# Two steps of a float64 unpacking on GpSimd and a scaling on ScalarE, in a recurrence and gated-MLP kernel whose order is written out by hand

## The chip, the cores and the metric

One core of a Trainium2 chip. The metric is the device time in microseconds of the whole kernel, the median of three runs. The engines are called PE (TensorE), DVE (VectorE), ACT (ScalarE), POOL (GpSimd) and SP (SyncE, which issues the DMAs here).

## The reference

Two parts follow each other. The first is a recurrence over 768 time steps for 4 batches of 8 heads, each with a 40 x 40 state. The second takes its output, 320 wide, through a projection to 1024, a convolution of three taps over time, a gate, and a projection back to 320:

```python
for t in range(S):                                   # S = 768; state is (B, H, 40, 40)
    y[:, :, t] = einsum("bhd,bhde->bhe", r_t, state)
    Sa = einsum("bhde,bhe->bhd", state, a_t)
    state = state * w_t[:, :, None, :] - einsum("bhd,bhe->bhde", Sa, b_t) \
            + einsum("bhd,bhe->bhde", v_t, k_t)
x = y.transpose(0, 2, 1, 3).reshape(B, S, 320)
h = maximum(x @ w_in, 0)                             # w_in: 320 x 1024
gate = 1 / (1 + exp(-conv3(h, conv_w)))              # three taps over time, per channel
out = (h * gate) @ w_out                             # w_out: 1024 x 320
```

w_in, conv_w and w_out lie in device memory as float64.

## The kernel before

**Recurrence.** Time is cut into 24 chunks of 32 steps, and two chunks make a pair (12 pairs). For a pair, the columns w, a, k, b are loaded and turned, a scan gives the decays, and `scores` gives the products within each chunk. `solve_in` sends them through DRAM into the layout bb, and `solve` (lines 480 and 486) inverts 32 x 32 triangular matrices, 128 of them at once, in 31 steps of two operations each: a product into st and a sum into xx. The even pairs' solves run on VectorE, the odd pairs' on GpSimd. `chain` then carries the state from chunk to chunk: TensorE's pp (L514, from the old state s and from v), ScalarE's psb (L527), TensorE's pu, ScalarE's u, TensorE's pn, the sum into the new s on VectorE (L562), and its scaling by wc in four operations on GpSimd (L568). For the outputs `rturn` makes rp (L579) and rt, `turn` makes vt and ut (L593), `sturn` makes sn, `pairs` takes pm (L411) into ms on VectorE (L614), `outputs` makes ysb, and `hats` makes khat and bhat (L451). `finish` splits the result in a high part xh (ScalarE) and a low part xl (GpSimd, L667).

**Second part.** It runs in 12 windows of 64 steps, each in four quarters of the 1024 channels (`moe_in`, `moe_out`), between the chunks of the recurrence. The matrix products are made of high and low parts too, so that each weight exists twice, as wih and wil (w_in) and as woh and wol (w_out).

**The weight pieces.** float64 is unpacked on the chip from its two 32-bit words, once, piece by piece, in 23 pieces: twelve of w_in (wi00 to wi23: the first digit is the group of 120 rows, the second the quarter of columns), one of conv_w (cv), eight of w_out (wo0 to wo7) and two for its last 64 columns (wp0, wp1). A piece is 120 or 128 partitions by 256 columns, cv 24 by 128. It has four steps: a load; `from_f64`, eight VectorE operations on integers (lines 217 to 235); the conversion to the high part on ScalarE (L253); the subtraction that gives the low part on GpSimd (L255). In `from_f64`, e holds the exponent, t the sign, the exponent and the upper mantissa, and m the remaining mantissa bits. Line 228 takes m out of the low word, line 230 clears t where the number is too small, line 231 (the mask) leaves in e only t's power of two, line 232 multiplies m, scaled by 2^-44, by that power, and line 235 adds the product to t. For cv a transposition on TensorE (pc, L269) takes the place of the last steps. The raw words lie in a buffer "gh", e and t in one half each of a buffer "gl" (named ...q in the trace), m in another "gl" (named ...s), with four buffers a tag. All weight pieces are built in the first third of the run, while solve 1 and solve 3 (pairs 1 and 3) run on GpSimd and solve 2 on VectorE.

**The order.** Nothing is reordered by a scheduler. A string ORDER lists the steps of all parts (`we3` is one step of weight piece 3, `so1` some steps of solve 1, `ch4` one step of the chain), `put` names which steps must stand ahead of which, and `emit_all` gives the steps out in that order. Each engine then works off its own queue strictly in order, and an instruction that waits holds everything behind it on its engine. ORDER is written on the level of steps: when a step has one more instruction on an engine, that instruction stands in the engine's queue where the step stands.

Of the kernel before, what the change touches and what calls it, by code (L numbers as in the profile page):

```python
# [8 lines left out]
F32 = mybir.dt.float32  # L9
# [3 lines left out]
AF = mybir.ActivationFunctionType  # L13
ALU = mybir.AluOpType
# [98 lines left out]
def tile_decay_delta_attention_then_conv_gate_moe(  # L113
# [13 lines left out]
    nc = tc.nc  # L127
# [30 lines left out]
    def quad(i):  # L158
        return slice(C * i, C * i + C)
# [7 lines left out]
        out=hmask, in_=hmask, compare_op=ALU.is_ge, fill=0.0,  # L167
# [3 lines left out]
        out=hmask, in_=hmask, compare_op=ALU.is_ge, fill=0.0,  # L171
# [4 lines left out]
    for q in range(B):  # L176
        nc.gpsimd.affine_select(
            out=tri[quad(q), :], in_=tri[quad(q), :],
# [6 lines left out]
        out=trin[:, 1, 0], in0=tri, scalar1=-1.0, scalar2=None, op0=ALU.mult  # L185
# [3 lines left out]
    for z in range(2):  # L189
        zs = slice(z * 64, z * 64 + 64)  # L190
        nc.gpsimd.affine_select(
            out=xini[zs], in_=xini[zs], compare_op=ALU.is_equal, fill=0.0,
# [20 lines left out]
    def from_f64(raw, e, t, m):  # L213

        lo, hi = raw[..., 0], raw[..., 1]
        V = nc.vector
        V.tensor_scalar(
            out=e, in0=hi, scalar1=20, scalar2=0x7FF,
            op0=ALU.logical_shift_right, op1=ALU.bitwise_and,
        )  # L220
        V.tensor_scalar(
            out=t, in0=hi, scalar1=3, scalar2=0x3FFFFFFF,
            op0=ALU.logical_shift_left, op1=ALU.bitwise_and,
        )
        V.scalar_tensor_tensor(
            out=t, in0=hi, scalar=-(1 << 30), in1=t, op0=ALU.bitwise_and, op1=ALU.bitwise_or
        )
        V.tensor_scalar(out=m, in0=lo, scalar1=8, scalar2=None, op0=ALU.logical_shift_right)
        tf, ef = t.bitcast(F32), e.bitcast(F32)
        V.scalar_tensor_tensor(out=tf, in0=e, scalar=896.5, in1=tf, op0=ALU.is_ge, op1=ALU.mult)  # L230
        V.tensor_scalar(out=e, in0=t, scalar1=-(1 << 23), scalar2=None, op0=ALU.bitwise_and)
        V.scalar_tensor_tensor(
            out=ef, in0=m, scalar=2.0**-44, in1=ef, op0=ALU.mult, op1=ALU.mult
        )
        V.tensor_tensor(tf, tf, ef, ALU.add)
        return tf

    def words(nm):
# [5 lines left out]
    def piece(nm, load, dsth, dstl, rows, shape):  # L244
        raw, e, t, m = words(nm)
        raw = raw[:rows]
        load(raw)
        yield
        f = from_f64(raw.rearrange("p (c z) -> p c z", z=2), e[:rows], t[:rows], m[:rows])
        if len(shape) == 2:  # L250
            f = f.rearrange("p (a c) -> p a c", a=shape[0])
        yield
        nc.scalar.copy(dsth, f)  # L253
        yield
        nc.gpsimd.tensor_tensor(dstl, f, dsth.bitcast(F32), ALU.subtract)  # L255
        yield

    def conv_piece():
        NCV = KW * NF
        craw, ce, ct, cm = words("cv")  # L260
        nc.sync.dma_start(craw[:NCV, :256], conv_w.rearrange("k (f p) -> (k f) p", p=256))
        yield
        cf = from_f64(
            craw[:NCV, :256].rearrange("p (c z) -> p c z", z=2),
            ce[:NCV, :128], ct[:NCV, :128], cm[:NCV, :128],
        )
        yield
        pc = psM.tile([128, 512], F32, tag="M", name="pc")
        nc.tensor.transpose(pc[:, :NCV], cf, ident[:NCV, :NCV])  # L269
        nc.scalar.copy(cw.rearrange("p k f -> p (k f)"), pc[:, :NCV])  # L270
        yield
        yield
# [730 lines left out]
```

## Time and profile before

| | |
|---|---|
| median of three runs | 711.65 us (707.79, 711.65, 715.09) |
| the profiled execution | 708.08 us, span 706.4 us |
| mean granted TensorE clock | 0.906 |
| TensorE, matmuls | 560.7 us busy, 79% of the span |
| VectorE | 538.4 us, 76% |
| ScalarE | 350.7 us, 50% |
| GpSimd | 353.2 us, 50% |
| data moved by DMA | 53.40 MB, 76 GB/s on average |

A row of a timeline gives the start in us from the span's start, the length of one instruction (or of a group, with xN), the engine, the line, the operation, its output and inputs with sizes, and in brackets the idle time of the engine just before it with what ended it. A row without brackets began as soon as its engine's previous instruction let it. A row of the stretches gives busy us of each engine with the number of instructions, the granted clock, the share of the DMA engines, and GB/s.

### The profile page before, as it was taken

Reading aid. Unit: us, or ns where it says so; the run is one execution under the profiler, and the core shown is the slowest. Engines: PE = TensorE matmul, PEld = TensorE weight load, DVE = VectorE, ACT = ScalarE, POOL = GpSimd, SP = SyncE. Lnnn points to the kernel's source line nnn. Section 1 sums busy time; section 2 is a strip of 40 time slices with the busy share of each in tenths; the row PEclk is TensorE's granted clock in tenths of the full one; section 3 lists DMA queues with packets and bytes.
Section 4 is the critical chain, followed back from the end, with each engine's and each line's share of the span. In section 5 each row is a group of like instructions: output and inputs, shape, how many; then the busy total and the mean of one; then the engine's idle time right before and its main releaser. Section 6 shows DMA issues by size and latency. Waiting matters only on the chain. (4 is left out here: it accounts for less than half of the span.)

```text
span 706.4 us, 29930 instructions
## 1 busy us (share of the span) xinstructions
PE 560.7 (79%) x13021; PEld 497.9 (70%) x13021; DVE 538.4 (76%) x1261; ACT 350.7 (50%) x792; POOL 353.2 (50%) x582
## 2 busy tenths in 40 slices
PE   4444764677687898988977996899998977899886
PEld 3334654566576787977866885789887876788775
DVE  6689889998999896657795578987979894456571
ACT  2322244254375455664454664466565546455651
POOL 2001884037786235783234884236985028863321
PEclk9766777997799998989999998999998999999998
DMA  8765456437125344544404446524435025121000
GB/s 139 120 117 108 103 112 102 95 94 144 22 41 107 56 72 79 94 81 82 82 20 89 86 86 106 81 60 69 89 62 91 6 54 94 29 51 32 21 30 19
DMA packets 242402, 53.40 MB, mean 76 GB/s; under 512 B 229000, under 2 KB 238112, under 8 KB 242272
## 3 DMA queue, kind: packets, MB, share of 16 engines
q1 hardware_dynamic: 242272, 51.50, 39.9%
q8 instruction: 102, 1.67, 1.0%
q14 instruction: 28, 0.23, 0.1%
HBM read 38.63 MB, written 10.22 MB: 69 GB/s over the span
## 5 line engine op out<-in xcount | busy, mean ns | idle before, releaser
L729 DVE SCALAR_TENSOR_TENSOR cc<-hb,cw,cc 128x256 f32<-128x256 f32 x192 | 106.3, 575 | 13.7 <-ACT cc L721 10.2
L568 POOL TENSOR_TENSOR s<-s,wc 120x360 f32<-120x360 f32 x88 | 75.8, 891 | 69.4 <-DVE s L562 69.4
L486 POOL TENSOR_TENSOR xx<-xx,st 128x126 f32<-128x126 f32 (+22 forms) x186 | 83.1, 447 | 14.6
L480 POOL TENSOR_TENSOR st<-xx,bb 128x126 f32<-128x126 f32 (+22 forms) x186 | 79.4, 427 | 21.1 <-DMA bb<-bd 8.4
L700 PE MATMUL ph<-xh,wih 120*128 120x256 f32 x288 | 56.6, 306 | 11.3 <-ACT hb L714 11.3
L486 DVE TENSOR_TENSOR xx<-xx,st 128x126 f32<-128x126 f32 (+22 forms) x186 | 54.2, 291 | 6.4
L480 DVE TENSOR_TENSOR st<-xx,bb 128x126 f32<-128x126 f32 (+22 forms) x186 | 53.6, 288 | 7.2 <-DMA bb<-bd 1.7
L736 DVE TENSOR_TENSOR cc<-cc,hb 128x512 f32<-128x512 f32 x48 | 40.8, 857 | 21.7 <-ACT cc L734 21.5
L562 DVE TENSOR_TENSOR s<-pn,s 120x360 f32<-120x360 f32 x88 | 40.6, 522 | 20.6 <-PE pn L549 20.6
L700 PEld LDWEIGHTS ph<-xh,wih 120*128 120x128 f32 x288 | 41.8, 194 | 15.0 <-ACT hb L714 13.1
L734 ACT ACTIVATE cc<-cc 128x512 f32<-128x512 f32 x48 | 30.4, 636 | 43.6 <-DVE cc L729 43.5
L667 POOL TENSOR_TENSOR xl<-xf,xh 120x384 fp32r<-120x384 f32 x24 | 26.8, 1117 | 45.2 <-ACT xh L665 41.5
L721 ACT ACTIVATE cc<-hb,cw 128x256 f32<-128x256 f32 x96 | 43.5, 506 | 8.7 <-DVE hb L712 2.9
L602 PE MATMUL pt<-ident,s 120*120 120x120 f32 x276 | 40.6, 279 | 6.4 <-DVE s L562 3.2
L427 ACT ACTIVATE ap<-ah,hmask 120x384 f32<-120x384 f32 (+1 forms) x72 | 36.6, 576 | 17.4 <-DVE ah L391 10.1
L604 ACT COPY sn<-pt 120x360 f32<-120x360 f32 x92 | 38.9, 471 | 12.2 <-PE pt L602 11.8
L714 ACT ACTIVATE hb<-ph 128x512 f32<-128x512 f32 x48 | 28.8, 600 | 27.2 <-PE ph L700 23.4
L579 ACT ACTIVATE rp<-pr,hmask 120x384 f32<-120x384 f32 x72 | 36.7, 586 | 6.9 <-PE pr L576 6.5
L700 PE MATMUL ph<-xl,wih 120*128 120x256 f32 x192 | 39.3, 287 | 0.0
L533 PE MATMUL pu<-psb,tt 32*32 32x40 f32 x1536 | 22.5, 209 | 19.6 <-ACT psb L527 16.1
L602 PEld LDWEIGHTS pt<-ident,s 120*120 120x120 f32 x276 | 31.2, 143 | 9.0 <-DVE s L562 3.5
L533 PEld LDWEIGHTS pu<-psb,tt 32*32 32x32 f32 x1536 | 18.7, 114 | 24.5 <-ACT psb L527 17.7
(867 smaller groups left out, 1665.9 us busy)
## 6 DMA issues: line engine op xcount, KB each, us to landing
bb<-bd SPq DMA_DIRECT2D x24, 256.0 KB
w<-in_w_dram SPq DMA_DIRECT2D x24, 160.0 KB
a<-in_a_dram SPq DMA_DIRECT2D x24, 160.0 KB
k<-in_k_dram SPq DMA_DIRECT2D x24, 160.0 KB
b<-in_b_dram SPq DMA_DIRECT2D x24, 160.0 KB
r<-in_r_dram SPq DMA_DIRECT2D x96, 40.0 KB
v<-in_v_dram SPq DMA_DIRECT2D x96, 40.0 KB
out_dram<-ob SPq DMA_DIRECT2D x22, 160.0 KB
```

The costliest lines, as they stand in the source:

```text
L480: eng.tensor_tensor(t3, xx[:, 0:nj, i : i + 1].to_broadcast([128, nj, nt]), bb[:, i : i + 1, i + 1 :].to_broadcast([128, nj, nt]), ALU.mult,)
L486: eng.tensor_tensor(xx[:, 0:nj, i + 1 :], xx[:, 0:nj, i + 1 :], t3, ALU.add)
L533: nc.tensor.matmul(pu[quad(bi), hc], tt[quad(bi), c, h, :], psb[quad(bi), hc], start=(h == 0), stop=True, skip_group_check=True,)
L562: nc.vector.tensor_tensor(new, pn[bi][:GR], old[bi], ALU.add)
L568: nc.gpsimd.tensor_tensor(n4, n4, w4, ALU.mult)
L579: nc.scalar.activation(out=rp[:, :, h, :], in_=pr[:GR], func=AF.Copy, scale=hmask[:, h : h + 1])
L602: nc.tensor.transpose(pt[:GR, g, :], old[bi][:, g, :], ident[:GR, :GR])
L604: nc.scalar.copy(sn, pt[:GR])
L700: nc.tensor.matmul(ph[:, j], l[:, fs], x, start=(j == 0 and i == 0), stop=(i == len(passes) - 1), skip_group_check=True,)
L721: nc.scalar.activation(out=cc[:, j], in_=hb[:, j, :, 1 : W + 1], func=AF.Copy, scale=cw[:, 1, f : f + 1],)
L729: nc.vector.scalar_tensor_tensor(out=cc[:, j], in0=hb[:, j, :, x : W + x], scalar=cw[:, x, f : f + 1], in1=cc[:, j], op0=ALU.mult, op1=ALU ...
L736: nc.vector.tensor_tensor(cc, cc, hb[:, :, :, 1 : W + 1], ALU.mult)
```

## The change

In `from_f64` the multiply and the add go from VectorE to GpSimd. GpSimd's multiply has two inputs only, so the factor 2^-44 becomes an operation of its own, on ScalarE, which also takes m from integer to float:

```diff
         V.tensor_scalar(out=m, in0=lo, scalar1=8, scalar2=None, op0=ALU.logical_shift_right)
         tf, ef = t.bitcast(F32), e.bitcast(F32)
+        nc.scalar.activation(out=m.bitcast(F32), in_=m, func=AF.Copy, scale=2.0**-44)
         V.scalar_tensor_tensor(out=tf, in0=e, scalar=896.5, in1=tf, op0=ALU.is_ge, op1=ALU.mult)
         V.tensor_scalar(out=e, in0=t, scalar1=-(1 << 23), scalar2=None, op0=ALU.bitwise_and)
-        V.scalar_tensor_tensor(
-            out=ef, in0=m, scalar=2.0**-44, in1=ef, op0=ALU.mult, op1=ALU.mult
-        )
-        V.tensor_tensor(tf, tf, ef, ALU.add)
+        nc.gpsimd.tensor_tensor(ef, m.bitcast(F32), ef, ALU.mult)
+        nc.gpsimd.tensor_tensor(tf, tf, ef, ALU.add)
         return tf
```

VectorE has six operations a piece instead of eight, ScalarE two instead of one, GpSimd three instead of one. Lines behind the change are numbered one less: L254, L479, L485 and L567 are the former L255, L480, L486 and L568. ORDER, the dependencies and the buffers are as before. The new instructions stand in their queues where the step `from_f64` of the piece stands in ORDER, two steps earlier than the subtraction of the same piece. Three places show it.

GpSimd's queue in the second half of solve 1, before (xx and st belong to the solve, wil to the pieces; the steps 12 to 19 that lie ahead are left out):

```order
L486 TENSOR_TENSOR xx_821<-xx_821,st_19_1165 128x10x12
L255 TENSOR_TENSOR wil<-wi22q,wih 120x256
L480 TENSOR_TENSOR st_20_1398<-xx_821,bb_673 128x121
L486 TENSOR_TENSOR xx_821<-xx_821,st_20_1398 128x11x11
L480 TENSOR_TENSOR st_21_1401<-xx_821,bb_673 128x110
```

The same place in the changed kernel:

```order
L485 TENSOR_TENSOR xx_827<-xx_827,st_19_1173 128x10x12
L233 TENSOR_TENSOR wi22q<-wi22s,wi22q 120x256
L234 TENSOR_TENSOR wi22q<-wi22q 120x256
L254 TENSOR_TENSOR wil<-wi22q,wih 120x256
L233 TENSOR_TENSOR wi03q<-wi03s,wi03q 120x256
L234 TENSOR_TENSOR wi03q<-wi03q 120x256
L233 TENSOR_TENSOR wi13q<-wi13s,wi13q 120x256
L234 TENSOR_TENSOR wi13q<-wi13q 120x256
L479 TENSOR_TENSOR st_20_1409<-xx_827,bb_679 128x121
L485 TENSOR_TENSOR xx_827<-xx_827,st_20_1409 128x11x11
```

Ahead of step 20 of the solve, where one subtraction stood, three pairs now stand as well, those of wi22, wi03 and wi13; further ahead, between steps 11 and 16, stand the pairs of wi02 and wi12.

ScalarE's queue in the same stretch, before, with the engine whose signal each instruction waits for (sn, ap, rp, rt, ut, ysb and khat belong to the recurrence):

```order
L253 CAST wih<-wi22q 120x256 [waits DVE_49]
L579 ACTIVATE rp_1235<-pr_1231,hmask 120x3x128 [waits PE_49]
L579 ACTIVATE rp_1235<-pr_1231,hmask 120x3x128 x2
L584 COPY rt_1239<-pr_1231 120x384
L604 COPY sn_1253<-pt_1249 120x360 [waits PE_49]
L604 COPY sn_1259<-pt_1255 120x360 [waits PE_49]
L593 COPY ut_1265<-put_1261 120x384 [waits PE_49,Activation_49]
L644 COPY ysb_1376<-py_1299 128x320 [waits PE_49,Activation_49]
L451 COPY khat_1378<-pz4k 128x320 [waits PE_49]
```

And in the changed kernel:

```order
L230 ACTIVATE wi22s<-wi22s 120x256 [waits DVE_49]
L252 CAST wih<-wi22q 120x256 [waits Pool_49]
L578 ACTIVATE rp_1244<-pr_1240,hmask 120x3x128 [waits PE_49]
L578 ACTIVATE rp_1244<-pr_1240,hmask 120x3x128 x2
L583 COPY rt_1248<-pr_1240 120x384
L230 ACTIVATE wi03s<-wi03s 120x256 [waits DVE_49]
L603 COPY sn_1263<-pt_1259 120x360 [waits PE_49]
L603 COPY sn_1269<-pt_1265 120x360 [waits PE_49]
L592 COPY ut_1275<-put_1271 120x384 [waits PE_49]
L643 COPY ysb_1386<-py_1309 128x320 [waits PE_49]
L450 COPY khat_1388<-pz4k 128x320 [waits PE_49]
L230 ACTIVATE wi13s<-wi13s 120x256 [waits DVE_49]
```

The conversion of wi22 waits for GpSimd instead of VectorE, ahead of rp and ut as before; the scaling of wi03 has come between rt and ut, that of wi13 behind khat.

GpSimd's queue in solve 3, four steps ahead of a scaling of the state (the xx and st of these rows belong to solve 3, wol and wo7 to the pieces), before:

```order
L480 TENSOR_TENSOR st_7_2730<-xx_2479,bb_2475 128x96
L486 TENSOR_TENSOR xx_2479<-xx_2479,st_7_2730 128x4x24
L255 TENSOR_TENSOR wol<-wo5q,woh 128x256
L480 TENSOR_TENSOR st_8_2814<-xx_2479,bb_2475 128x115
L486 TENSOR_TENSOR xx_2479<-xx_2479,st_8_2814 128x5x23
```

And in the changed kernel:

```order
L479 TENSOR_TENSOR st_7_2750<-xx_2497,bb_2493 128x96
L485 TENSOR_TENSOR xx_2497<-xx_2497,st_7_2750 128x4x24
L254 TENSOR_TENSOR wol<-wo5q,woh 128x256
L233 TENSOR_TENSOR wo7q<-wo7s,wo7q 128x256
L234 TENSOR_TENSOR wo7q<-wo7q 128x256
L479 TENSOR_TENSOR st_8_2835<-xx_2497,bb_2493 128x115
L485 TENSOR_TENSOR xx_2497<-xx_2497,st_8_2835 128x5x23
```

Behind these rows steps 8 to 11 of solve 3 and then the four scalings of the state (L568, now L567) follow in both kernels. The pair of wo7 stands ahead of them now; it can run only when VectorE has done wo7's six operations and ScalarE its scaling.

## The prediction

> **What bounds the kernel now.** I read the page's first part, then busy time by stage, then each engine's timeline through the first 240 us, where all weight pieces are built. Over the span no engine is full:
>
> ```profile
> PE 560.7 (79%) x13021; PEld 497.9 (70%) x13021; DVE 538.4 (76%) x1261; ACT 350.7 (50%) x792; POOL 353.2 (50%) x582
> ```
>
> By stage it is otherwise (columns: stretch, its length, then busy us of each engine):
>
> ```profile
> core 0: us, PE busy (x) PEld busy (x) DVE busy (x) ACT busy (x) POOL busy (x), PEclk, DMA share, GB/s
> 53.70:74.00 20.30, 11.33 (x290) 9.77 (x282) 19.41 (x49) 4.42 (x11) 5.83 (x10) 0.61 0.63 116
> 74.00:101.40 27.40, 19.02 (x569) 16.20 (x569) 23.74 (x53) 8.88 (x22) 23.95 (x52) 0.75 0.54 110
> 101.40:126.90 25.50, 12.65 (x234) 10.99 (x232) 22.27 (x51) 10.67 (x25) 12.25 (x20) 0.78 0.50 97
> 126.90:149.40 22.50, 17.44 (x563) 15.08 (x563) 20.48 (x71) 10.29 (x24) 4.61 (x7) 0.92 0.44 97
> 149.40:199.80 50.40, 37.25 (x991) 32.01 (x991) 46.36 (x102) 21.80 (x51) 33.09 (x58) 0.80 0.38 75
> 400.00:500.00 100.00, 88.04 (x2104) 79.79 (x2101) 81.29 (x185) 58.28 (x132) 57.85 (x91) 0.97 0.48 80
> ```
>
> From 53.7 to 199.8 VectorE is busy 132.3 of 146.1 us (91%) and sets the pace; later TensorE does (88%). So a delay at 200 us is carried to the end, and VectorE time saved before 200 us could be a gain. But GpSimd, the average's idle engine, is busy 23.95 of 27.40 us in the second row: solve 1 runs on it there, and solve 3 in the fifth row (33.09 us). The moved pairs join its queue in just these stretches.
>
> **The change part by part: durations.** Four answers give the busy time of one line over the first 240 us (stretch, length, busy us with the number of instructions, then the clock and DMA columns). The two removed VectorE lines, 232 (the multiply) and 235 (the add):
>
> ```profile
> 0.00:240.00 240.00, 10.90 (x23) 0.82 0.53 99
> ...
> 0.00:240.00 240.00, 10.31 (x23) 0.82 0.53 99
> ```
>
> The nearest GpSimd operation, line 255 (the subtraction, the same 256 columns, two inputs), and the nearest ScalarE one, line 253 (the conversion, 256 columns):
>
> ```profile
> 0.00:240.00 240.00, 17.65 (x22) 0.82 0.53 99
> ```
> ```profile
> 0.00:240.00 240.00, 9.04 (x22) 0.82 0.53 99
> ```
>
> VectorE loses 10.90 + 10.31 = 21.2 us, 0.92 a piece. GpSimd gains 46 operations at 17.65/22 = 0.80, 36.9 us; with an estimated 0.05 of hand-over I count 1.65 a pair. ScalarE gains 23 x 9.04/22 = 9.4 us, 0.41 a piece. No row shows the GpSimd multiply or add or the ScalarE scaling itself. From the rows quoted below a pair lies between 0.92 (two solve steps of 121 columns at 0.46) and 2.06 (two xl subtractions of 384 columns at 1.03), the scaling between 0.41 and 0.53 (the copy ut); I take 1.65 and 0.41, from the rows of the same size. Over a queue of three pairs the bounds mean -2.2 to +1.2 us. The memory is the same and no DMA is issued differently. So the cost is in the order: the conversion now waits for GpSimd's pair instead of VectorE's add, and the pair stands in GpSimd's queue among solve steps.
>
> **Link 1, GpSimd reaches piece wi22 late.** GpSimd in solve 1, and ScalarE around it:
>
> ```profile
> 71.08 0.24 POOL L480 TENSOR_TENSOR st<-xx,bb 128x31 f32<-128x31 f32 x1 [5.59 <-DMA bb<-bd]
> ...
> 93.91 0.78 POOL L255 TENSOR_TENSOR wil<-wi22q,wih 120x256 fp32r<-120x256 f32 x1
> 94.66 0.46 POOL L480 TENSOR_TENSOR st<-xx,bb 128x121 f32<-128x121 f32 x1
> ...
> 104.96 0.77 POOL L486 TENSOR_TENSOR xx<-xx,st 128x16 f32<-128x16 f32 x1
> 105.68 1.00 POOL L667 TENSOR_TENSOR xl<-xf,xh 120x384 fp32r<-120x384 f32 x1
> ...
> 107.33 4.36 POOL L568 TENSOR_TENSOR s<-s,wc 120x360 f32<-120x360 f32 x4
> ...
> 112.49 1.03 POOL L667 TENSOR_TENSOR xl<-xf,xh 120x384 fp32r<-120x384 f32 x1
> ```
> ```profile
> 92.18 0.41 ACT L253 CAST wih<-wi22q 120x256 fp32r<-120x256 f32 x1 [3.15 <-DVE wi22q L235]
> 92.49 1.52 ACT L579 ACTIVATE rp<-pr,hmask 120x384 f32<-120x384 f32 x3
> ...
> 94.95 0.53 ACT L593 COPY ut<-put 120x384 f32<-120x384 f32 x1
> ...
> 101.54 0.42 ACT L451 COPY khat<-pz4k 128x320 f32<-128x320 f32 x1 [0.28 <-PE pz4k L450]
> ```
>
> From 71.08, when a transfer lets solve 1 begin, GpSimd has no wait until it is done. Its 93.91 moves by the pairs of wi02, wi12 and wi22 (3 x 1.65) and one hand-over to ScalarE for wi12 (0.5): 99.4. The conversion of wi22, at 92.18 now, then starts at 99.4: +7.2, and behind it in ScalarE's queue stand rp and, with the scaling of wi03 (0.4) put in between, ut: 102.6 instead of 94.95.
>
> **Link 2, VectorE stands still and GpSimd waits for it.** Who waits for ut, and later for conv's piece and for the chain's psb:
>
> ```profile
> 95.53 1.08 PE L411 MATMUL pm<-rp,ut 120*32 120x96 f32 x24 [0.38 <-ACT ut L593]
> ...
> 117.96 0.30 PE L269 MATMUL pc<-ident,cvq 24*128 24x24 f32 x1 [7.85 <-DVE cvq L235]
> ```
> ```profile
> 97.62 0.68 DVE L614 TENSOR_TENSOR ms<-pm,tri 128x512 f32<-128x512 f32 x1
> ...
> 126.90 0.42 DVE L473 CAST xx<-xini 128x512 f32<-128x512 bf16 x1
> ```
> ```profile
> 127.33 0.43 ACT L527 ACTIVATE psb<-pp 128x320 f32<-128x320 f32 x1
> ```
>
> VectorE's ms comes after pm, at 102.6 + 0.5 + 1.1 = 104.2 instead of 97.62; the next thing in VectorE's queue is piece wi13, so that comes 6.6 late too. Its scaling stands in ScalarE's queue behind ysb and khat, which follow ms: khat ended 4.34 us after ms began (101.96 - 97.62), so 108.5, the scaling ends at 108.95, the pair at 110.6. Behind the pair stand the last eleven steps of solve 1 (94.66 to 105.73, 11.1 us): 121.7, +16. Behind these the xl, the s scalings of the state and the second xl (105.68 to 113.52, 7.8 us): 129.5; then the pairs of wi23 and of conv (1.65 + an estimated 0.9 at half the columns): 132.0. TensorE's pc, which waited for conv's piece until 117.96, waits till 132.0 (+14), and with it all TensorE work behind it, the transposes that VectorE needs before wo1. VectorE reaches solve 2 (126.90) some 13 us late after its saving in wo1, ScalarE psb (127.33) some 14. While VectorE stands still GpSimd may run up to 2 us faster, as the pair of VectorE rows under the rivals suggests; I take **+12** for this stage, bounds +9 and +15.
>
> **Link 3, the state's scaling in solve 3.** Around piece wo7:
>
> ```profile
> 168.05 0.29 DVE L217 TENSOR_SCALAR wo5q<-wo5r 128x256 int32<-128x256 int32 x1 [1.45 <-DMA wo5r<-in_moe_w_out_dram]
> ...
> 187.43 0.43 DVE L231 TENSOR_SCALAR wo7q<-wo7q 128x256 int32<-128x256 int32 x1
> ```
> ```profile
> 174.82 1.03 POOL L480 TENSOR_TENSOR st<-xx,bb 128x115 f32<-128x115 f32 x1
> ...
> 180.08 3.71 POOL L568 TENSOR_TENSOR s<-s,wc 120x360 f32<-120x360 f32 x4 [0.26 <-DVE s L562]
> ```
> ```profile
> 184.73 0.79 PE L522 MATMUL pp<-v,at 32*32 32x40 f32 x64
> ```
> ```profile
> 189.10 0.41 ACT L253 CAST woh<-wo7q 128x256 fp32r<-128x256 f32 x1 [5.74 <-DVE wo7q L235]
> ...
> 189.78 0.44 ACT L527 ACTIVATE psb<-pp 128x320 f32<-128x320 f32 x1
> ```
>
> In the new order the pair of wo7 stands ahead of the solve steps that began at 174.82 and of the s scalings. I count in the clock of the kernel before, all of it shifted by link 2. VectorE gave wo7's last mask at 187.43. It saves 0.92 on each of wo2 to wo6, but it stands waiting in this stage too (1.45 us for wo5's load alone), so the mask comes at 187.3 or up to 3 us earlier. With 187.3 the pair ends at 188.95, the four steps (174.82 to 179.83, 5.0) at 193.95, the s scalings (3.71) at 197.66 instead of 183.79. TensorE's pp ended 1.73 us behind them (185.52), so at 199.4. Before, psb was read only at 189.78, since ScalarE stood before wo7's conversion, and 199.4 is 9.6 later. I take **+9** at psb, and +6 if the mask is 3 us earlier.
>
> After 200 us GpSimd lags the rest by 4 to 5 us more:
>
> ```profile
> 218.67 3.71 POOL L568 TENSOR_TENSOR s<-s,wc 120x360 f32<-120x360 f32 x4
> ```
> ```profile
> 227.79 0.76 PE L514 MATMUL pp<-s,ah 120*32 120x120 f32 x24
> ```
>
> The scalings end at 222.4 and are used at 227.8, so 5.4 us of slack hide that. From there TensorE's 88% give nothing back.
>
> **The sum.** +12 + 9 = +21. The profiled execution took 708.08 us (span 706.4), so 729; that execution lies 3.6 below the median 711.65 of three, which would give 733. I say **731**.
>
> **The rivals.** *VectorE's saving counts (faster).* VectorE is 91% busy from 53.7 to 199.8 and loses about 19.4 us of work there; at that share 17, at most 15 after the new hand-overs: 697. For it: the table. Against it: GpSimd has no idle time between 71.08 and 93.91. It decides from the point where GpSimd's pair of wi22 is done by 92.2, when VectorE's add is now: three pairs would have to cost nearly nothing, or steps of solve 1 be that much faster beside an emptier VectorE. Chance 0.10.
>
> *Delays are caught up (within 1%).* Transfers run ahead while the engines wait, and VectorE, with 0.92 less a piece, closes up from 127 to 200: of 12 only 8 stay, and s is hidden behind the 4.2 us of slack at psb and the earlier mask: +4, 715. Against it: ScalarE's and GpSimd's queues are strict, and neither had a gap to close in links 1 and 2. Chance 0.14.
>
> *The port costs more (slower still).* VectorE's line 221 took, with GpSimd idle and with GpSimd in solve 1:
>
> ```profile
> 15.18 0.28 DVE L221 TENSOR_SCALAR wi00q<-wi00r 120x256 int32<-120x256 int32 x1
> ...
> 94.03 0.82 DVE L221 TENSOR_SCALAR wi03q<-wi03r 120x256 int32<-120x256 int32 x1
> ```
>
> Each of the 46 new GpSimd operations may hold a VectorE operation by that 0.54; where VectorE sets the pace and GpSimd was not busy anyway, about 22 of them, this adds 12: 743. Against it: in links 1 and 2 VectorE stands still anyway. Chance 0.08. The Trainium skill, page SBUF — State Buffer, section "Who interferes with whom", says that VectorE and GpSimd share a port pair as an exclusive lock, the loser waiting for the whole instruction. By that rule the held operation waits up to the 0.80 of the GpSimd row, so 22 x 0.80 = 18 and 749; the two rows above agree in kind and show less.
>
> **How the numbers follow.** Forecast 0.68: both delays, 718 (+9 and nothing at s, from the median less 3) to 742 (+15, +10 and a little of the port). The range goes down to 714 to take in the delays that are caught up; what it leaves out is the faster rival and the port's upper part. One per cent (7.1 us) is about what a measurement of this kernel can tell from no change. Faster by over that 0.10, within it 0.14, slower 0.68 + 0.08 = 0.76.
>
> **What would show it.** In the profile after: ScalarE's conversions of wi12 and wi22 wait on GpSimd's new pair, not on VectorE; ms 6 to 7 us later; solve 1's last step near 121; pc near 132; solve 2 on VectorE 11 to 14 us late; the s scalings after solve 3's steps behind wo7's pair. Wrong would be: solve 1 done by 114, pc waiting for nothing, or VectorE fuller than 91% up to the last piece.

## The result, and the profile after

The changed kernel takes 735.8 us (median of four runs, 733.7 to 737.3) against 710.2 us (four executions of the kernel before; the first three alone gave 711.65): ratio 1.0375, 95% interval 1.0333 to 1.0418, 26 us slower. Its profiled execution took 737.3 us, span 735.6. The first part of its page, busy time over the span:

```profile
PE 568.2 (77%) x13021; PEld 504.1 (69%) x13021; DVE 524.2 (71%) x1215; ACT 358.9 (49%) x815; POOL 382.6 (52%) x628
```

VectorE has 14 us less to do, GpSimd 29 us more, and neither is full. Then busy time by stage. The stretches are the same in time as before, and the changed kernel runs late, so its later rows hold work that stood in earlier ones. The changed kernel comes first, then the one row of the kernel before that has not been shown yet:

```profile
core 0: us, PE busy (x) PEld busy (x) DVE busy (x) ACT busy (x) POOL busy (x), PEclk, DMA share, GB/s
74.00:101.40 27.40, 14.46 (x388) 12.12 (x388) 15.84 (x35) 9.66 (x25) 22.40 (x44) 0.75 0.40 80
101.40:126.90 25.50, 11.14 (x296) 9.31 (x296) 15.70 (x31) 9.24 (x23) 18.88 (x34) 0.63 0.36 75
149.40:199.80 50.40, 37.03 (x992) 32.49 (x980) 36.75 (x93) 22.71 (x52) 26.08 (x44) 0.86 0.46 97
199.80:226.30 26.50, 16.12 (x384) 12.48 (x382) 12.86 (x30) 9.97 (x26) 20.22 (x36) 0.71 0.01 3
```
```profile
199.80:226.30 26.50, 21.53 (x460) 19.01 (x460) 24.85 (x46) 15.57 (x36) 20.14 (x33) 1.00 0.46 88
```

VectorE, 91% busy before 200 us, is now busy 15.84 of 27.40 and 15.70 of 25.50 us: it waits. From 199.8 to 226.3 it is busy for half the stretch (24.85 us before), and DMA has all but stopped (0.01; 0.46 before). So the question for each engine is what it waits for.

Links 1 and 2, in the order in which the delay runs. ScalarE, then VectorE:

```profile
97.95 0.41 ACT L252 CAST wih<-wi22q 120x256 fp32r<-120x256 f32 x1 [4.75 <-POOL wi22q L234]
```
```profile
102.75 0.69 DVE L613 TENSOR_TENSOR ms<-pm,tri 128x512 f32<-128x512 f32 x1 [4.68 <-PE pm L410]
```

GpSimd, which then waits in the middle of solve 1, and its last step:

```profile
106.97 0.74 POOL L233 TENSOR_TENSOR wi13q<-wi13s,wi13q 120x256 f32<-120x256 f32 x1 [4.89 <-ACT wi13s L230]
107.78 1.25 POOL L234 TENSOR_TENSOR wi13q<-wi13q 120x256 f32<-120x256 f32 x1
109.00 0.40 POOL L479 TENSOR_TENSOR st<-xx,bb 128x121 f32<-128x121 f32 x1
...
119.89 0.23 POOL L485 TENSOR_TENSOR xx<-xx,st 128x16 f32<-128x16 f32 x1
```

And TensorE and ScalarE behind it:

```profile
129.35 0.30 PE L268 MATMUL pc<-ident,cvq 24*128 24x24 f32 x1 [5.20 <-POOL cvq L234]
```
```profile
139.61 0.40 ACT L252 CAST woh<-wo1q 128x256 fp32r<-128x256 f32 x1 [2.01 <-POOL wo1q L234]
139.92 0.43 ACT L526 ACTIVATE psb<-pp 128x320 f32<-128x320 f32 x1
```

The bracket names the next link each time: the conversion waits for GpSimd, ms for TensorE, wi13's pair for a scaling that follows ms, pc for GpSimd. psb of chunk 2 is 12.6 us late (127.33 before). It stands behind the conversion of wo1, which waits for GpSimd too; TensorE's pp was done 2.9 us before psb began (137.02), and 2.3 us in the kernel before.

The psb of every chunk serves as a clock for the whole; the table gives its start before, and how much later it is in the kernel after.

| chunk | 2 | 3 | 4 | 5 | 6 | 8 | 12 | 23 |
|---|---|---|---|---|---|---|---|---|
| psb before, us | 127.3 | 145.6 | 166.9 | 189.8 | 231.0 | 269.4 | 374.8 | 647.3 |
| after, later by | 12.6 | 13.3 | 12.9 | 23.7 | 26.5 | 26.0 | 25.6 | 27.5 |

The loss arises in two steps, before chunk 2 and between chunks 4 and 6, and almost nothing is given back. Link 3, the second step: ScalarE, VectorE, GpSimd, ScalarE and VectorE again.

```profile
188.90 0.42 ACT L230 ACTIVATE wo6s<-wo6s 128x256 f32<-128x256 int32 x1 [2.33 <-DVE wo6s L228]
...
191.35 0.49 ACT L537 COPY u<-pu 128x320 f32<-128x320 f32 x1
```
```profile
195.51 1.85 DVE L561 TENSOR_TENSOR s<-pn,s 120x360 f32<-120x360 f32 x4 [5.98 <-PE pn L548]
```
```profile
202.19 0.72 POOL L233 TENSOR_TENSOR wo7q<-wo7s,wo7q 128x256 f32<-128x256 f32 x1 [7.01 <-DVE wo7q L232]
...
207.80 3.05 POOL L567 TENSOR_TENSOR s<-s,wc 120x360 f32<-120x360 f32 x4
```
```profile
213.46 0.44 ACT L526 ACTIVATE psb<-pp 128x320 f32<-128x320 f32 x1 [8.93 <-PE pp L521]
```
```profile
217.64 0.80 DVE L217 TENSOR_SCALAR wp1q<-wp1r 128x256 int32<-128x256 int32 x1 [12.10 <-POOL wol L254]
```

GpSimd stands 7.0 us for wo7's mask with solve 3 and the state's scaling behind it; psb stands 8.9 us for them; and VectorE stands 12.1 us for a buffer that GpSimd frees with a subtraction; this one waits for ScalarE's conversion of wo6, which stands behind psb and u. Something else shows too: the scaling of wo6 on ScalarE waits 2.3 us for VectorE, ahead of u.

### The profile page after: what moved, and what is told of

The parts are those of the page before. It is cut to its first block, busy times and chain, and to the rows that moved or that the text cites. A ratio compares the mean times of both kernels' runs of the same rounds, so it can differ in the third digit from the quotient of the medians.

```text
span 735.6 us, 29983 instructions
## 1 busy us (share of the span) xinstructions
PE 568.2 (77%) x13021; PEld 504.1 (69%) x13021; DVE 524.2 (71%) x1215; ACT 358.9 (49%) x815; POOL 382.6 (52%) x628
## 5 line engine op out<-in xcount | busy, mean ns | idle before, releaser
L567 POOL TENSOR_TENSOR s<-s,wc 120x360 f32<-120x360 f32 x88 | 74.5, 877 | 57.5 <-DVE s L561 57.5
L485 POOL TENSOR_TENSOR xx<-xx,st 128x126 f32<-128x126 f32 (+22 forms) x186 | 83.6, 449 | 14.6
L479 POOL TENSOR_TENSOR st<-xx,bb 128x126 f32<-128x126 f32 (+22 forms) x186 | 75.2, 404 | 17.5 <-DMA bb<-bd 4.8
L699 PE MATMUL ph<-xh,wih 120*128 120x256 f32 x288 | 57.6, 310 | 10.8 <-ACT hb L713 10.8
L479 DVE TENSOR_TENSOR st<-xx,bb 128x126 f32<-128x126 f32 (+22 forms) x186 | 54.7, 294 | 6.9 <-DMA bb<-bd 1.4
L485 DVE TENSOR_TENSOR xx<-xx,st 128x126 f32<-128x126 f32 (+22 forms) x186 | 54.3, 292 | 6.4
L426 ACT ACTIVATE ap<-ah,hmask 120x384 f32<-120x384 f32 (+1 forms) x72 | 36.6, 576 | 16.9 <-DVE ah L390 10.5
L666 POOL TENSOR_TENSOR xl<-xf,xh 120x384 fp32r<-120x384 f32 x24 | 25.2, 1051 | 36.6 <-ACT xh L664 32.9
```

The costliest lines, as they stand in the source:

```text
L479: eng.tensor_tensor(t3, xx[:, 0:nj, i : i + 1].to_broadcast([128, nj, nt]), bb[:, i : i + 1, i + 1 :].to_broadcast([128, nj, nt]), ALU.mult,)
L485: eng.tensor_tensor(xx[:, 0:nj, i + 1 :], xx[:, 0:nj, i + 1 :], t3, ALU.add)
L567: nc.gpsimd.tensor_tensor(n4, n4, w4, ALU.mult)
L699: nc.tensor.matmul(ph[:, j], l[:, fs], x, start=(j == 0 and i == 0), stop=(i == len(passes) - 1), skip_group_check=True,)
```

## The experiments

**Theory (order):** the cost is where the new instructions stand in strict queues: pairs on GpSimd ahead of steps of solve 1 and of the state's scaling. **Rival (amount):** the cost is the GpSimd work itself, spread over all pieces. **Rival (ScalarE):** the scaling in ScalarE's queue is what holds everything up. Runs e1, e2, e5 to e9, e11 and e12 change a chosen set of pieces and leave the others as before:

```diff
+        moved = nm in (...)
+        if moved:
+            nc.scalar.activation(out=m.bitcast(F32), in_=m, func=AF.Copy, scale=2.0**-44)
...
+        if moved:
+            nc.gpsimd.tensor_tensor(ef, m.bitcast(F32), ef, ALU.mult)
+            nc.gpsimd.tensor_tensor(tf, tf, ef, ALU.add)
+        else:
             V.scalar_tensor_tensor(
                 out=ef, in0=m, scalar=2.0**-44, in1=ef, op0=ALU.mult, op1=ALU.mult
             )
             V.tensor_tensor(tf, tf, ef, ALU.add)
```

All results together. The ratio is to the kernel before on the same chip; the last columns are how late psb is in the one profiled execution of each. Medians of the kernel before ran from 708.3 to 711.3 us beside the different runs, so the ratios are to be compared. Single executions of one kernel lie up to 11 us apart; the profiled one is the fastest of e4's and e6's, and the slowest of the change's, e1's, e2's and e7's.

| run: changed | median us | ratio (95%) | chunk 2 | 4 | 5 | 6 |
|---|---|---|---|---|---|---|
| the change: all 23 | 735.8 | 1.0375 (1.0333 to 1.0418) | 12.6 | 12.9 | 23.7 | 26.5 |
| e1: five in solve 1 | 720.2 | 1.0154 (1.0117 to 1.0190) | 9.0 | 9.8 | 10.4 | 10.6 |
| e2: wo7 | 715.8 | 1.0077 (1.0045 to 1.0109) | 0.2 | 1.2 | 7.1 | 7.6 |
| e3: the add alone, all | 721.7 | 1.0172 (1.0131 to 1.0213) | 5.8 | 5.9 | 12.5 | 13.3 |
| e4: the scaling alone, all | 718.5 | 1.0137 (1.0092 to 1.0181) | 0.8 | 1.0 | 5.8 | 7.2 |
| e5: wi02, wi12, wi22 | 714.6 | 1.0040 (1.0001 to 1.0079) | 4.3 | 4.7 | 4.2 | 5.3 |
| e6: wi03, wi13 | 713.5 | 1.0035 (1.0009 to 1.0060) | 3.7 | 6.1 | 4.2 | 4.8 |
| e7: all but six | 717.5 | 1.0103 (1.0068 to 1.0137) | 1.2 | 1.9 | 5.6 | 8.1 |
| e8: eleven outside | 708.0 | 0.9967 (0.9930 to 1.0003) | -0.8 | 1.1 | 1.0 | 0.8 |
| e9: wo6 | 715.6 | 1.0098 (1.0060 to 1.0135) | -0.4 | -0.2 | 3.6 | 3.4 |
| e10: all, a step later | 736.1 | 1.0392 (1.0344 to 1.0439) | 14.3 | 13.8 | 22.0 | 27.5 |
| e11: six early | 709.1 | 0.9991 (0.9961 to 1.0021) | -0.5 | -0.3 | -1.4 | -1.0 |
| e12: six and two | 709.9 | 1.0009 (0.9981 to 1.0038) | -0.5 | 0.3 | -0.6 | -0.9 |

**e1.** `moved = nm in ("wi02", "wi12", "wi22", "wi03", "wi13")`.

> Only the five pieces built while solve 1 runs on GpSimd (wi02, wi12, wi22, wi03, wi13) are changed; the other 18 keep VectorE's multiply and add. Theory (order): the cost is where the pairs stand in GpSimd's queue, so these five give what the changed kernel showed up to chunk 2, +11 to +13 us (about 722), with solve 1's last step near 120 and psb of chunk 2 some 12 late, and nothing after that. Rival (amount): the 26 us are spread over all pieces as GpSimd work and as contention with VectorE, so five of 23 give +5 to +6 us (716).

Ratio 1.0154, about 11 us for five of 23 pieces; by amount it would be 5 to 6. GpSimd stands in the same place as in the kernel after, and the state's scaling behind solve 1 starts at 122.5 (107.3 before):

```profile
107.60 0.73 POOL L236 TENSOR_TENSOR wi13q<-wi13s,wi13q 120x256 f32<-120x256 f32 x1 [5.56 <-ACT wi13s L232]
...
122.52 3.10 POOL L576 TENSOR_TENSOR s<-s,wc 120x360 f32<-120x360 f32 x4
```

After chunk 2 nothing is added (9.0, 9.8, 10.4, 10.6). What the kernel after has more at chunk 2, 3.6 us, belongs to other pieces. pc starts at 126.54 in e1, as soon as VectorE has done conv's piece, and at 129.35 in the kernel after, where it waits for the pairs of wi23 and of conv on GpSimd (126.39 to 129.29): 2.8 us. The other 0.8 arise at wo1, whose pair stands ahead of the conversion in front of psb.

**e2.** `moved = nm == "wo7"`.

> Only piece wo7 is changed. Theory (order): its pair stands ahead of four steps of solve 3 and of the state's scaling, so the scaling starts some 13 us late and psb of chunk 5 +9 to +11 us (about 720) from this one piece. Rival (amount): one of 23 pieces gives +1 us, no change that can be measured.

One piece of 23 costs 0.77%, 5.5 us, five times what amount would give, and less than the 9 to 11 expected. GpSimd:

```profile
185.29 0.72 POOL L236 TENSOR_TENSOR wo7q<-wo7s,wo7q 128x256 f32<-128x256 f32 x1 [8.12 <-DVE wo7q L234]
...
191.21 3.04 POOL L576 TENSOR_TENSOR s<-s,wc 120x360 f32<-120x360 f32 x4
```

The state's scaling is 11.1 us late (180.08 before), psb of chunk 5 only 7.1, since before psb was read 4.3 us after pp was ready (189.78 against 185.52). That is the slack that the prediction counted; the place is right, and here VectorE gave wo7 2 us earlier than I had put it.

**e3.** In all pieces the factor and the multiply stay on VectorE:

```diff
         V.scalar_tensor_tensor(
             out=ef, in0=m, scalar=2.0**-44, in1=ef, op0=ALU.mult, op1=ALU.mult
         )
-        V.tensor_tensor(tf, tf, ef, ALU.add)
+        nc.gpsimd.tensor_tensor(tf, tf, ef, ALU.add)
```

> In all pieces only the last add goes to GpSimd; the multiply with its factor stays on VectorE, and ScalarE gets no scaling. Theory (order): the place in the queue decides, not the number of operations: the adds of wi13 and wo7 still stand ahead of the solve steps and wait for VectorE, so most of the loss stays, +16 to +23 us (about 730), a few us less than with the pair because each place is 0.85 us shorter and no scaling stands behind khat. Rival (amount): half of the moved operations give half of the loss, +13 us (723).

Ratio 1.0172, 12 us: less than the 16 to 23 that order gave, and near the rival's 13. The places are the expected ones, only shorter. GpSimd in solve 1 and in solve 3:

```profile
102.68 0.73 POOL L235 TENSOR_TENSOR wi13q<-wi13q 120x256 f32<-120x256 f32 x1 [5.16 <-DVE wi13q L232]
...
191.47 0.72 POOL L235 TENSOR_TENSOR wo7q<-wo7q 128x256 f32<-128x256 f32 x1 [4.71 <-DVE wo7q L232]
```

wi13's add waits until 102.68 where the pair waited until 106.97: ms is 2.1 us late instead of 5.1, and no scaling stands between VectorE and GpSimd. Whether ScalarE's scaling is part of the loss, the next run shows; it takes it alone.

**e4.** ScalarE scales, VectorE multiplies and adds:

```diff
+        nc.scalar.activation(out=m.bitcast(F32), in_=m, func=AF.Copy, scale=2.0**-44)
...
-        V.scalar_tensor_tensor(
-            out=ef, in0=m, scalar=2.0**-44, in1=ef, op0=ALU.mult, op1=ALU.mult
-        )
+        V.tensor_tensor(ef, m.bitcast(F32), ef, ALU.mult)
         V.tensor_tensor(tf, tf, ef, ALU.add)
```

> In all pieces ScalarE scales m, but the multiply and the add stay on VectorE as two operations: VectorE has eight operations as before, GpSimd one. Theory (order on GpSimd): GpSimd's queue is as before, VectorE now waits for ScalarE's scaling in some pieces, so 0 to +8 us (about 715). Rival (ScalarE): the scaling in ScalarE's strict queue is what holds everything up, so +18 us or more (over 728).

Ratio 1.0137, 9 to 10 us (8 between the medians), just above the 0 to 8 of the theory and half of what the rival needs. It is not spread: psb is on time to chunk 4 (+1.0) and 5.8 us late at chunk 5. ScalarE there, with u at 176.13 before:

```profile
178.65 0.42 ACT L232 ACTIVATE wo6s<-wo6s 128x256 f32<-128x256 int32 x1 [3.71 <-DVE wo6s L228]
178.97 0.46 ACT L601 COPY vt<-pvt 120x384 f32<-120x384 f32 x1
179.33 1.18 ACT L612 COPY sn<-pt 120x360 f32<-120x360 f32 x3
...
181.10 0.49 ACT L546 COPY u<-pu 128x320 f32<-128x320 f32 x1
```

A scaling of 0.42 us stands ahead of vt, sn and u and waits 3.7 us for wo6's mantissa bits; u is 5.0 us late, and VectorE's sum into s with it. The ScalarE rival is right at this one place. The 9 to 10 us are not the scaling's share of the change, for here VectorE also waits for scalings ahead of its multiply (2.76 us at wo5), which it doesn't in the change.

**e5 and e6: links 1 and 2 apart.** `moved = nm in ("wi02", "wi12", "wi22")`, and `moved = nm in ("wi03", "wi13")`.

> Only wi02, wi12 and wi22 are changed: link 1 alone. Theory: their three pairs stand ahead of wi22's conversion, ScalarE reaches rp and ut about 5 us late, ms +5 us, solve 1's end +5, psb of chunk 2 and the whole about +5 us (715 to 716). Rival (the loss in solve 1 comes from the pair of wi13, which waits for VectorE): +1 us or less here.

> Only wi03 and wi13 are changed: link 2 alone. Theory: ms is not late, but the pair of wi13 waits in GpSimd's queue for ScalarE's scaling behind khat (ended 101.96), so that the last eleven steps of solve 1 begin at about 104 instead of 94.7 and end near 115 (+9); the slack behind them (in the run with five pieces +15 at the state's scaling gave +9 at psb of chunk 2) leaves +3 to +4 us (714). Rival (only the late ms of link 1 counts): 0 to +1 us.

In e5 ms starts at 102.7 (97.62 before, +5.1), and psb of chunk 2 is 4.3 us late; the time is up 0.40%, 3 us. In e6 ms is on time (+0.3) and GpSimd waits all the same:

```profile
102.26 0.73 POOL L236 TENSOR_TENSOR wi13q<-wi13s,wi13q 120x256 f32<-120x256 f32 x1 [4.85 <-ACT wi13s L232]
...
115.45 0.23 POOL L494 TENSOR_TENSOR xx<-xx,st 128x16 f32<-128x16 f32 x1
```

Solve 1's last step is 10.5 us late, psb of chunk 2 is 3.7, the time up 0.35%, 2.5 us. Both rivals, that one link alone counts, fall by psb (the times alone, with intervals that begin at 0.01% and 0.09%, would hardly decide): 4.3 and 3.7 add up to nearly the 9.0 of the five pieces. The times of the two add up to less (0.75% of 1.54%). In the profiled executions that difference arises behind chunk 6 (psb of chunk 23 is 5.1 late in e5, on time in e6, 13.7 late in e1); it was not followed.

**e7.** `moved = nm not in ("wi02", "wi12", "wi22", "wi03", "wi13", "wo7")`.

> All pieces are changed but wi02, wi12, wi22, wi03, wi13 and wo7. Theory: what is left of the loss sits at three places: the scaling of wo6 on ScalarE ahead of u of chunk 4 (about +2 to +5 us, seen in the run with ScalarE's scaling alone), the pairs of wi23 and the convolution piece behind solve 1 (+2 to +3), the pairs of wp0 and wp1 ahead of the end of solve 3 (+3): +7 to +11 us (719). Rival (the six pieces are the whole loss): 0 to +2 us.

Ratio 1.0103, 7 us, as forecast, and the rival (0 to 2) falls. Two of the three places show. u of chunk 4 is 4.0 us late (wo6). And psb of chunk 6 is 2.5 us later than that of chunk 5: with the pairs of wp0 and wp1 in its queue GpSimd takes up the next step of solve 3 only 9.1 us after psb of chunk 5 begins, as in the kernel after; before it was 4.9 us. The third does not: pc, which waits for the convolution's piece, is on time (117.96 in both). That place costs only when solve 1 is late already. The three parts e1, e2 and e7 add up to 3.3% against 3.75% for the whole.

**e8.** `moved = nm in ("wi00", "wi10", "wi20", "wi01", "wi11", "wi21", "wo0", "wo1", "wo2", "wo3", "wo4")`.

> Only the eleven pieces wi00 to wi21 and wo0 to wo4 are changed, which are built while GpSimd has little to do. Theory: nothing stands behind their pairs, VectorE saves 10 us in these stretches, but the end of each is set by a transfer or by the chain, so -2 to +1 us (709 to 711). Rival (VectorE sets the pace there): -5 to -10 us (about 702), which would beat the kernel before.

22 GpSimd operations and 11 scalings, about half of the change, cost nothing: 0.9967, with no change inside the interval. By amount they would cost 12 us. VectorE's busy time falls in this run too, for instance from 46.36 to 43.68 of the 50.40 us that begin at 149.4:

```profile
149.40:199.80 50.40, 38.48 (x1009) 32.36 (x1001) 43.68 (x95) 22.73 (x54) 37.51 (x63) 0.80 0.36 75
```

So the work that the eleven pieces take off VectorE, 10 us by the 0.92 a piece, brings 2 us (at most 5 by the interval, at least nothing), though VectorE was 91% busy there before: it is not the one that sets the end of these stages.

**e9.** `moved = nm == "wo6"`.

> Only piece wo6 is changed. Theory: wo6 has two places of its own, its scaling on ScalarE ahead of u of chunk 4 (u +5 us) and its pair on GpSimd ahead of steps 4 to 11 of solve 3 and the state's scaling (pair done near 180.7, scaling of the state near 190, +10); both end at the same psb of chunk 5, +5 to +6 us (716), as much as wo7 alone gave, so the two do not add. Rival (amount): one of 23 pieces gives +1 us.

Ratio 1.0098, 7 us, one piece again; amount is out. psb of chunk 5 is 3.6 us late in the profiled execution, less than expected, since u is 2.0 late instead of 5 (VectorE reached wo6 earlier there: the scaling at 175.65) and the state's scaling 6.1 instead of 10. psb stands behind the conversion of wo7 there, which waits for VectorE, and so for u; pp was done 1.0 us earlier. wo6 and wo7 each cost 5 to 7 us alone; the whole change loses 11 us between chunks 4 and 5.

**e10.** Scaling and pair are given out one step of the piece later:

```diff
+        def rest():
+            nc.scalar.activation(out=m.bitcast(F32), in_=m, func=AF.Copy, scale=2.0**-44)
+            nc.gpsimd.tensor_tensor(ef, m.bitcast(F32), ef, ALU.mult)
+            nc.gpsimd.tensor_tensor(tf, tf, ef, ALU.add)
+        return tf, rest
...
         yield
+        rest()
         nc.scalar.copy(dsth, f)
```

> All pieces are changed, with the same instructions on each engine, but ScalarE's scaling and GpSimd's pair are given out one step of the piece later, directly ahead of the conversion: the pairs of wi03 and wi13 then stand behind solve 1, wo6's scaling behind u, wo7's pair behind the four solve steps (still ahead of the state's scaling). Theory (place): ms stays +5 late from wi22, ScalarE waits for wi13's pair behind solve 1 (ap +9, psb of chunk 2 about +8), psb of chunk 5 another +5: +10 to +17 us (724). Rival (amount: the same work gives the same loss wherever it stands): +24 us or more (735).

Ratio 1.0392: no better than the change, and my 10 to 17 us was wrong. Solve 1 does end 8 us earlier than in the kernel after, but ScalarE now stands where GpSimd stood. GpSimd's last step, ScalarE and VectorE:

```profile
111.94 0.23 POOL L490 TENSOR_TENSOR xx<-xx,st 128x16 f32<-128x16 f32 x1
```
```profile
113.67 0.40 ACT L256 CAST wih<-wi13q 120x256 fp32r<-120x256 f32 x1 [4.23 <-POOL wi13q L236]
...
117.44 0.41 ACT L256 CAST wih<-wi03q 120x256 fp32r<-120x256 f32 x1 [1.64 <-POOL wi03q L236]
```
```profile
117.55 0.69 DVE L441 TENSOR_TENSOR at<-ps,trin 128x512 f32<-128x512 f32 x1 [5.33 <-PE ps L415]
```

The conversion of wi13 (102.64 before) stands 11 us late in front of ScalarE's ap, TensorE's ps and VectorE's product with trin. I had taken the delay of ap with the slack that e1 showed behind solve 1; on this path there is none: VectorE's wi23 starts 11.4 us late (123.07) behind it, pc, with the pairs of wi23 and of conv ahead of it, 13.2 us late (131.18), and psb of chunk 2 14.3. By its total this run would fit the amount rival too; e1, e2, e8 and e9 rule that out.

**e11 and e12.** The six pieces ahead of solve 1, and these with wo0 and wo1.

> Only the six pieces built before solve 1 are changed. Theory: solve 1's start is set by a transfer, so the 5.5 us that VectorE saves give -2 to +1 us (709 to 711). Rival (VectorE sets the pace): -4 us or more (706).

> The six early pieces and wo0, wo1, which are built while GpSimd waits 14 us for the chain. Theory: -3 to 0 us (708 to 711), a gain at most near what can be measured. Rival (the saving counts in full): -7 us (703).

0.9991 and 1.0009: no change that can be measured. No version here is shown to beat the kernel before; e8 is the nearest.

## Why the prediction was right, and where it was off

731 us with 714 to 742 was forecast, 735.8 measured; slower by over 1% had 0.76. Against the profiled execution the sum was +21, measured +26.5 at psb of chunk 6 and +25.6 between the medians. The mechanism was the forecast one at all three links; what was missed stands below, and errors in link 3 cancel in part.

- **Link 1 held.** wi22's conversion was forecast for 99.4 and began at 97.95; ms for 104.2, began at 102.75. e5 shows it alone.
- **Link 2 held.** Pair of wi13 done by 110.6, measured 109.0; solve 1's end 121.7, measured 120.1; pc 132, measured 129.35; solve 2 on VectorE some 13 late, measured 10.8 (137.72); psb some 14, measured 12.6. The +12 for this stage was the right size. Its working gave 14, and 2 were taken off because GpSimd might run faster beside an idle VectorE. That came true in part: the last eleven steps of solve 1 took 11.1 us in both kernels, the row of work behind them (xl to second xl) 6.4 instead of 7.8. e6 shows that it needs no late ms.
- **Durations held.** Over the first 270 us 23 multiplies took 17.25 us and 23 adds 19.43, so a pair is 1.59 us (1.65 taken); the scaling is 9.53/23 = 0.41, as taken.
- **Link 3 was right in its place and too small.** +9 forecast (9.6 by its working), 23.7 - 12.9 = 10.8 measured. The term that failed is the mask of wo7, "at 187.3 or up to 3 us earlier" in the clock of before. It ended at 202.04 where 187.3 + 12.9 = 200.2 would have been on time: 1.8 us later, since VectorE stood 5.98 us for pn, and pn for u. Two other terms were too long and one too short: the four solve steps took 4.1 instead of 5.0 us, the scalings 3.05 instead of 3.71, but pp ended 2.55 us behind them instead of 1.73. 9.6 + 1.8 - 0.9 - 0.7 + 0.8 gives 10.6, near the 10.8; that nearly half of the mask's lateness was made good is luck.
- **A late u was missing.** Of the new scalings on ScalarE the prediction counts only those of wi03 and wi13, and wo6's not at all. That one waits for VectorE ahead of u, which comes 5.0 us late in e4 and 2.0 in e9; this is why the mask of wo7 was late.
- **The slack after 200 us did not hide the rest.** From chunk 5 to chunk 6 another 2.8 us are lost (23.7 to 26.5), 2.5 in e7, and 0.2 and 0.5 in e1 and e2, which leave wp0 and wp1 alone. I had looked at the state's scaling alone, where 5.4 us are free. Not in the sum were the pairs of wp0 and wp1 ahead of solve 3's next steps (9.1 us behind psb instead of 4.9) and the scaling of wp1 ahead of ysb on ScalarE, which waits 2.8 us for VectorE (ysb 7.2 us behind psb instead of 6.0). Which of the two counts more was not separated: e3, which has the add alone, loses 0.8 us there, e4, which has the scaling alone, 1.4, and e5, which leaves both pieces alone, 1.1, so that single executions do not tell these apart. VectorE's wait of 12.1 us is no loss of its own: in e7 it is 1.08 us, and the 2.5 us are lost all the same.
- **The rivals.** VectorE's saving counts: hardly, by e8's 0.9967 it is 2 us where nothing stands against it, 5 at most. Caught up: no, 12.6, 13.3, 12.9 over chunks 2 to 4. (Its working does not add up: where 8 of 12 us stay and s is hidden, the sum is +8 and 720, not +4 and 715.) The port: the six VectorE operations that stay took 57.6 us in 23 pieces before and 61.5 after, 3.9 us together, and 3.0 of these at conv's piece. All that stays on VectorE grew by 7.0 us (21.2 us were removed, and it is busy 14.2 less). That rival asked for 12; its estimate by the lock of which the Trainium skill (SBUF — State Buffer, "Who interferes with whom") speaks was 18. The runs show less than both.

## What to carry to other kernels

Where each engine works off its queue strictly in order, an operation moved to an idle engine costs what stands behind it while it waits, more than its length: 0.42 us of ScalarE ahead of u held u back by 2 to 5 us (e9, e4), and eleven whole pieces at places with nothing behind them cost nothing that could be measured. Before moving work, list for every new instruction what it waits for and who waits for the instruction behind it, on all engines it touches, also for those that seem free. Moving the instruction later in the program is no remedy by itself: e10 gave back GpSimd's 8 us and lost them on ScalarE.

## What the runs showed of the hardware

The granted TensorE clock was lower in two of the stretches above: 0.63 instead of 0.78 between 101.4 and 126.9 us, and 0.71 instead of 1.00 between 199.8 and 226.3. It did not follow TensorE's waiting everywhere: from 74.0 to 101.4 it was 0.75 in both kernels, though TensorE was busy 14.46 instead of 19.02 us, and from 149.4 to 199.8 it was 0.86 instead of 0.80. Over the whole run it was 0.889 instead of 0.906. Between 205 and 214 us it was 0.50, and the 64 products of pp with v took 1.29 us there (at 212.10) where they took 0.79 before (at 184.73, clock 1.00). How much of the 26 us comes by way of the clock was not separated.

GpSimd's four scalings of the state took 3.05 us at 207.80 in the kernel after, where VectorE stood waiting all the while, and 3.71 at the same place before (180.08), where VectorE was busy. The other way round, VectorE's six operations on conv's piece (24x128) took 0.70 to 0.99 us each in the kernel after, with GpSimd at work beside them, 4.92 in all; before, they took 1.92 in all, five of them 0.21 to 0.28 each.
